# Group normalization on one core: a one-tile VectorE loop, a quartered last store, and longer runs of stores and loads

## The chip, the cores and the metric

The kernel runs on 1 core of a Trainium2 chip. The metric is the time of one execution on the device, in microseconds (us). Kernels are compared only within the same rounds.

Beside the profile page and its views I use two kinds of records that lie in the same trace: one for each packet that a DMA engine moved (start, duration, size), and one for each of the 16 completions that a transfer reports. "us as a mean of 16" means that the engines' lost times were added and divided by 16.

## The reference

```python
# x: [128, 1024, 32, 16] bf16; g, b: [1024] bf16; 32 groups of 32 channels
xr  = x.reshape(B, 32, C // 32, H, W)
mu  = xr.mean(axis=(2, 3, 4), keepdims=True)
var = ((xr - mu) ** 2).mean(axis=(2, 3, 4), keepdims=True)
xn  = (xr - mu) / jnp.sqrt(var + 1e-5)
return xn.reshape(B, C, H, W) * g[None, :, None, None] + b[None, :, None, None]
```

One (image, group) pair fills one partition with 16384 values. A tile is 128 such pairs, 4 MB, and there are 32 tiles. Each is loaded once and stored once: 134 MB in, 134 MB out.

## The kernel before

Six tiles (slots) lie in SBUF at a time. SyncE issues all loads and stores on one queue, in runs: two stores, then two loads, then three and three.

```python
def on_sync(e):
    def load(j):                       # needs the slot's last store to have landed
        if j >= SLOTS:
            e.wait_ge(st[j % SLOTS], 16 * (j // SLOTS))
        e.dma_start(out=slot(j), in_=x_v[j]).then_inc(ld[j % SLOTS], 16)
    def store(i):                      # needs VectorE to have finished the tile
        e.wait_ge(done[i % SLOTS], i // SLOTS + 1)
        e.dma_start(out=o_v[i], in_=slot(i)).then_inc(...)
    for j in range(SLOTS):
        load(j)
    for i in range(NT):
        store(i)
        if i % RUN == FIRST_RUN - 1:   # RUN = 3, FIRST_RUN = 2
            for j in range(max(SLOTS, i + 1 + SLOTS - RUN), min(i + 1 + SLOTS, NT)):
                load(j)
```

For each tile TensorE sums 12 of 32 chunks, VectorE sums the other 20 by pairs ("the pair sum"; for the last tile TensorE sums all 32 and VectorE none), ScalarE forms the mean and then the squares, and VectorE normalizes in place with 32 instructions. VectorE's loop is unrolled over the six slots, with fixed addresses:

```python
def one(c, turn):                      # VectorE
    ...
    if follows:
        pair(*then)                    # pair sum of the next tile, waits for its load
    e.wait_ge(stded[c], turn)
    ...                                # 1/std, scale, bias: three small instructions
    for k in range(KC):                # 32 x tensor_scalar, 128 x 512
        ...
    ts.then_inc(done[c], 1)            # releases the store
```

## Time and profile before

| | before |
|---|---|
| time, median of the first 3 runs | 632.77 us (632.59 to 633.53) |
| span of the profiled execution | 630.3 us |
| data moved | 268.48 MB |
| duration of a 32 KB packet, at the 1st and at the 90th percentile | 1.213 us |
| VectorE per tile when it does not wait | 16.55 us |
| load plus store of a tile at the steady rate | 19.4 us |

These lines are from the page of the kernel before: the span, each engine's busy time with its share of the span, then, over 40 slices of 15.8 us, the mean busy share of the 16 DMA engines in tenths and what they moved in GB/s, and the share of the DMA queues.

```profile
span 630.3 us, 2508 instructions
...
PE 157.6 (25%) x405; PEld 52.0 (8%) x405; DVE 522.3 (83%) x1185; ACT 504.0 (80%) x258; POOL 0.8 (0%) x6
...
DMA  8999999999999999999999999999999999999996
GB/s 366 433 431 416 433 433 434 430 433 435 435 435 433 430 433 433 435 433 435 433 433 428 433 433 426 433 433 437 430 433 433 433 428 433 433 433 429 433 410 285
...
q1 hardware_dynamic: 9216, 268.44, 99.0%
```

VectorE is busy for 83% of the span, ScalarE for 80%, and the DMA engines for 99%. The rate stands at 433 GB/s in nearly every slice. No 32 KB packet of this trace took less than 1.213 us. The 8192 of them are 512 for each of the 16 engines, which is 621.1 us at 1.213 us each; with a first packet at 2.0 us there is little left to win while packets take that long.

One tile in VectorE's timeline (start, duration, instruction, count):

```profile
51.45 0.20 DVE L253 RECIPROCAL rstd<-std 128x1 f32<-128x1 f32 x1
51.69 0.24 DVE L255 TENSOR_SCALAR scl<-gb,rstd 128x32 f32<-128x32 f32 x1
51.96 0.25 DVE L259 SCALAR_TENSOR_TENSOR bia<-scl,nm,gb 128x32 f32<-128x32 f32 x1
52.25 10.43 DVE L268 TENSOR_SCALAR ring<-ring,scl,bia 128x512 bf16<-128x512 bf16 x32
62.59 5.49 DVE L236 SCALAR_TENSOR_TENSOR jp<-ring 128x5120 fp8e5<-128x5120 bf16 x1
```

The pair sum of the next tile starts at 62.59, before the last normalizing instruction has ended at 62.68: there is no gap between tiles.

The end, in the view of windows (from, to, length, busy us and instruction count of each engine, clock, DMA share, GB/s):

```profile
605.00:610.00 5.00, 0.00 (x0) 0.00 (x0) 4.76 (x16) 0.10 (x1) 0.00 (x0) 0.50 1.03 446
610.00:615.00 5.00, 0.00 (x0) 0.00 (x0) 5.00 (x17) 0.00 (x0) 0.00 (x0) 0.50 0.74 321
615.00:620.00 5.00, 0.00 (x0) 0.00 (x0) 1.33 (x5) 0.00 (x0) 0.00 (x0) 0.50 0.80 341
620.00:625.00 5.00, 0.00 (x0) 0.00 (x0) 0.00 (x0) 0.00 (x0) 0.00 (x0) 0.50 0.99 426
```

There is a dip from 613.5 to 617.5 us, worth 2.55 us as a mean of 16: the last tile is finished at 616.4 and most engines have nothing to store before that. But the 16 completions of one transfer are spread over 0.7 us at the beginning of the execution and over 5.5 us at the end. The store before the last is complete on the median engine at 614.2 us and on the slowest at 619.4. The slowest one has no dip, and it ends the execution.

### The profile page before, as it was taken

Reading aid. Unit: us, or ns where it says so; the run is one execution under the profiler, and the core shown is the slowest. Engines: PE = TensorE matmul, PEld = TensorE weight load, DVE = VectorE, ACT = ScalarE, POOL = GpSimd, SP = SyncE. Lnnn points to the kernel's source line nnn. Section 1 sums busy time; section 2 is a strip of 40 time slices with the busy share of each in tenths; the row PEclk is TensorE's granted clock in tenths of the full one; section 3 lists DMA queues with packets and bytes.
Section 4 is the critical chain, followed back from the end, with each engine's and each line's share of the span. In section 5 each row is a group of like instructions: output and inputs, shape, how many; then the busy total and the mean of one; then the engine's idle time right before and its main releaser. Section 6 shows DMA issues by size and latency. Waiting matters only on the chain.

```text
span 630.3 us, 2508 instructions
## 1 busy us (share of the span) xinstructions
PE 157.6 (25%) x405; PEld 52.0 (8%) x405; DVE 522.3 (83%) x1185; ACT 504.0 (80%) x258; POOL 0.8 (0%) x6
## 2 busy tenths in 40 slices
PE   1453205005302320250052015203510450065000
PEld 0110001001100100010010001001100110012000
DVE  1579999999996998599589949994997799499671
ACT  0799999999996999399859958993999399769930
POOL 0000000000000000000000000000000000000000
PEclk9867656556655665665566556655665665567555
DMA  8999999999999999999999999999999999999996
GB/s 366 433 431 416 433 433 434 430 433 435 435 435 433 430 433 433 435 433 435 433 433 428 433 433 426 433 433 437 430 433 433 433 428 433 433 433 429 433 410 285
DMA packets 9316, 268.48 MB, mean 426 GB/s; under 512 B 1120, under 2 KB 1120, under 8 KB 1120
## 3 DMA queue, kind: packets, MB, share of 16 engines
q1 hardware_dynamic: 9216, 268.44, 99.0%
q8 instruction: 1, 0.02, 0.0%
q14 instruction: 3, 0.02, 0.0%
q10 hardware_dynamic: 96, 0.00, 0.0%
HBM read 134.22 MB, written 134.22 MB: 426 GB/s over the span
## 4 chain that ended last, share of the span: by engine, by line
DMA 63%; DVE 26%; ACT 7%; issue 0%; SPq 0%; DVEq 0%
DMA out_dram<-ring 43%; DMA ring<-in_x_dram 20%; DVE ring L268 16%; DVE jp L236 9%; ACT ja L203 7%; DVE bia L259 0%; DVE scl L255 0%; ACT jm L195 0%; SPq L123 0%; ACT var L213 0%; DVE rstd L253 0%; ACT std L217 0%; DVEq L275 0%; SPq L309 0%; SPq L278 0%
## 5 line engine op out<-in xcount | busy, mean ns | idle before, releaser
L203 ACT ACTIVATE ja<-ring,nm 128x8192 fp8e5<-128x8192 bf16 x64 | 455.9, 7123 | 2.1
L268 DVE TENSOR_SCALAR ring<-ring,scl,bia 128x512 bf16<-128x512 bf16 x1024 | 333.7, 408 | 1.2
L173 PE MATMUL ps<-ring,eye 128*128 128x512 bf16 x404 | 157.4, 571 | 411.8 <-DMA ring<-in_x_dram 411.8
L236 DVE SCALAR_TENSOR_TENSOR jp<-ring 128x5120 fp8e5<-128x5120 bf16 x31 | 170.1, 5488 | 63.8 <-DMA ring<-in_x_dram 63.8
L195 ACT ACTIVATE jm<-ps 128x513 fp8e5<-128x513 f32 (+1 forms) x32 | 19.2, 601 | 95.0 <-DVE jp L236 95.0
L173 PEld LDWEIGHTS ps<-ring,eye 128*128 128x128 bf16 x404 | 51.9, 134 | 516.9 <-issue 467.2
L253 DVE RECIPROCAL rstd<-std 128x1 f32<-128x1 f32 x32 | 6.3, 198 | 15.5 <-ACT std L217 15.5
L203 ACT ACTIVATION_READ_ACCUMULATOR ja<-ring,nm 128x1 f32 x64 | 12.0, 187 | 0.0
L217 ACT ACTIVATE std<-sq,var 128x1 f32<-128x1 f32 x32 | 9.4, 295 | 1.0
L213 ACT ACTIVATE var<-sq,eps_t 128x1 f32<-128x1 f32 x32 | 9.4, 295 | 1.0
L259 DVE SCALAR_TENSOR_TENSOR bia<-scl,nm,gb 128x32 f32<-128x32 f32 x32 | 8.0, 251 | 1.1
L255 DVE TENSOR_SCALAR scl<-gb,rstd 128x32 f32<-128x32 f32 x32 | 7.7, 241 | 1.1
L231 DVE COPY gb<-gb_p 128x64 f32<-128x64 f32 x1 | 0.2, 225 | 10.1 <-PE gb_p L167 10.1
L195 ACT ACTIVATION_READ_ACCUMULATOR jm<-ps 128x1 f32 x32 | 6.2, 194 | 0.0
L236 DVE DVE_READ_ACCUMULATOR jp<-ring 128x1 f32 x31 | 4.4, 143 | 0.0
L167 PE MATMUL gb_p<-gb_b,rep 32*128 32x64 bf16 x1 | 0.2, 205 | 11.2 <-DMA gb_b<-in_b_dram 11.2
L188 ACT ACT_TABLE_LOAD x1 | 1.3, 1283 | 1.9 <-issue 1.9
L224 DVE MEMSET ones_b<- 128x128 bf16 x1 | 0.2, 165 | 1.1 <-SPq L278 1.1
L167 PEld LDWEIGHTS gb_p<-gb_b,rep 32*128 32x128 bf16 x1 | 0.1, 100 | 11.1 <-issue 11.1
L146 POOL TENSOR_SCALAR_AFFINE_SELECT rep<-ones_b 32x128 bf16<-32x128 bf16 x1 | 0.3, 304 | 0.0
L142 POOL TENSOR_SCALAR_AFFINE_SELECT eye<-ones_b 128x128 bf16<-128x128 bf16 x1 | 0.3, 295 | 0.9 <-DVEq L226 0.9
L188 ACT ACTIVATE warm<-eps_t 128x1 f32<-128x1 f32 x1 | 0.2, 203 | 0.0
(5 smaller groups left out, 0.5 us busy)
## 6 DMA issues: line engine op xcount, KB each, us to landing
ring<-in_x_dram SPq DMA_DIRECT2D x32, 4096.0 KB, 29.1
out_dram<-ring SPq DMA_DIRECT2D x32, 4096.0 KB, 33.9
gb_b<-in_g_dram ACTq DMA_DIRECT2D x1, 2.0 KB, 6.4
gb_b<-in_b_dram ACTq DMA_DIRECT2D x1, 2.0 KB, 9.6
```

Of the source, the lines that this page charges most:

```text
L167: e.matmul(out=gb_p[:], lhsT=rep[:], rhs=gb_b[:], start=True, stop=True).then_inc(s_gbp, 1)
L173: mm = e.matmul(out=sums(c), lhsT=eye[:], rhs=slot(c)[:, k * MM_FREE : (k + 1) * MM_FREE], start=(k == 0), stop=(k == chunks - 1),)
L188: e.activation(out=warm[:], in_=eps_t[:], func=ACT.Sqrt)
L195: e.activation(out=jm[:, 0 : src.shape[1]], in_=src, func=ACT.Identity, scale=-inv_n, accum_out=nm[:, c : c + 1], saturate=False,).then_in ...
L203: e.activation(out=ja[:], in_=slot(c)[:, h * (F // 2) : (h + 1) * (F // 2)], func=ACT.Square, bias=nm[:, c : c + 1], scale=1.0, accum_out= ...
L213: e.activation(out=var[:], in_=sq[:, 0:1], func=ACT.Identity, bias=eps_t[:], scale=inv_n).then_inc(varred[c], 1)
L217: e.activation(out=std[:, c : c + 1], in_=sq[:, 1:2], func=ACT.Sqrt, bias=var[:], scale=inv_n).then_inc(stded[c], 1)
L236: e.scalar_tensor_tensor(out=jp[:], in0=slot(c)[:, first : first + w], scalar=1.0, in1=slot(c)[:, first + w : first + 2 * w], op0=ALU.mult ...
L253: e.reciprocal(out=rstd[:], in_=std[:, c : c + 1]).then_inc(inverted[c], 1)
L255: e.tensor_scalar(out=scl[:], in0=gb[:, 0:KC], scalar1=rstd[:], scalar2=None, op0=ALU.mult).then_inc(scaled[c], 1)
L259: e.scalar_tensor_tensor(out=bia[:], in0=scl[:], scalar=nm[:, c : c + 1], in1=gb[:, KC : 2 * KC], op0=ALU.mult, op1=ALU.add,).then_inc(shi ...
L268: ts = e.tensor_scalar(out=a, in0=a, scalar1=scl[:, k : k + 1], scalar2=bia[:, k : k + 1], op0=ALU.mult, op1=ALU.add,)
```

## The change

Its intent: VectorE's loop shrinks to one tile, with the addresses of the 32 normalizing instructions computed in registers ahead of time, under the pair sum; the last store goes out in quarters, so that it starts before the tile is complete; and stores and loads alternate in longer runs, so that the queue changes direction (from loads to stores or back) less often. ScalarE and TensorE are looped in full too, TensorE's last matmul waits for the pair sum, and the pair sum waits for TensorE's first matmul instead of the load. The last tile is now treated like the others, with a pair sum on VectorE.

```diff
-TRIPS = 5
-RUN = 3
-FIRST_RUN = 2
+RUNS = (3, 4, 4, 4, 4, 4, 3, 6)
+NQ = 4
...
         def store(i):
-            e.wait_ge(done[i % SLOTS], i // SLOTS + 1)
-            e.dma_start(out=o_v[i], in_=slot(i)).then_inc(
-                st[i % SLOTS] if i + SLOTS < NT else s_fin, 16
-            )
+            w = F // store_parts(i)              # 4 parts for the last tile, else 1
+            for p in range(store_parts(i)):
+                e.wait_ge(done, NQ * i + NQ // store_parts(i) * (p + 1))
+                e.dma_start(
+                    out=o_v[i][:, p * w : (p + 1) * w], in_=slot(i)[:, p * w : (p + 1) * w]
+                ).then_inc(st[i % SLOTS] if i + SLOTS < NT else s_fin, 16)
...
-        for i in range(NT):
-            store(i)
-            if i % RUN == FIRST_RUN - 1:
-                for j in range(max(SLOTS, i + 1 + SLOTS - RUN), min(i + 1 + SLOTS, NT)):
-                    load(j)
+        i = 0
+        for run in RUNS:
+            for n in range(run):
+                store(i + n)
+            i += run
+            for j in range(i + SLOTS - run, min(i + SLOTS, NT)):
+                load(j)
...                                              # VectorE
-        pair(0, 1)
-        e.drain()
-        in_rounds(e, one)
+        pair(0)
+        with nc.Fori(0, NT, 1, engines=[e.engine]) as i:
+            with e.If(i < NT - 1):
+                e.drain()
+                pair(i + 1)
+            parts = [part(i, k * HW, HW) for k in range(KC)]
+            e.keepalive_nop([e.lower_ap(a) for a in parts])
+            e.wait_ge(stded, i + 1)
...
+            for k, a in enumerate(parts):
                 ts = e.tensor_scalar(
                     out=a, in0=a, scalar1=scl[:, k : k + 1], scalar2=bia[:, k : k + 1],
                     op0=ALU.mult, op1=ALU.add,
                 )
-            ts.then_inc(done[c], 1)
+                if (k + 1) % KQ == 0:
+                    ts.then_inc(done, 1)
```

More of the change, by code (lines that the diff above doesn't have):

```diff
@@ L53 @@
     NMM = F // MM_FREE
-    LOOPED = TRIPS * SLOTS
+    ROUNDS = -(-NT // SLOTS)
+    REST = NT - (ROUNDS - 1) * SLOTS
+    KQ = KC // NQ
     PAIRED = F - PE_CHUNKS * MM_FREE
-    assert SLOTS < NT and LOOPED < NT - 1 and NT - LOOPED <= SLOTS
+    ITEM = 2
+    assert NT > SLOTS and 0 < REST < SLOTS and sum(RUNS) == NT and RUNS[-1] == SLOTS
     assert F % MM_FREE == 0 and PAIRED % 2 == 0 and SLOTS % PS_BUFS == 0
@@ L94, in sems @@
         return [sem(f"{name}{c}") for c in range(SLOTS)]
-    ld, st, summed, paired, meaned, stded, done = (
-        sems(n) for n in ("ld", "st", "sum", "pair", "mean", "std", "done")
-    )
-    half, both, varred, inverted, scaled, shifted = (
-        sems(n) for n in ("half", "both", "var", "inv", "scl", "bia")
-    )
+    ld, st, summed, meaned = (sems(n) for n in ("ld", "st", "sum", "mean"))
+    half, both, varred = (sems(n) for n in ("half", "both", "var"))
+    inverted, scaled, shifted = (sem(n) for n in ("inv", "scl", "bia"))
+    first_in, paired, stded, done = (sem(n) for n in ("first", "pair", "std", "done"))
     s_gb, s_ones, s_eye, s_gbp, s_fin = (
@@ L105, with store_parts @@
     )
+    def store_parts(i):
+        return NQ if i == NT - 1 else 1
     def slot(i):
@@ L114, in sums_and_pairs @@
         return ps[:, c % PS_BUFS * 2 * MM_FREE : c % PS_BUFS * 2 * MM_FREE + MM_FREE + 1]
-    def pairs(c):
-        return ps[:, (c % PS_BUFS * 2 + 1) * MM_FREE : (c % PS_BUFS * 2 + 1) * MM_FREE + 1]
     def on_sync(e):
@@ L125, in store @@
         def store(i):
-            e.wait_ge(done[i % SLOTS], i // SLOTS + 1)
-            e.dma_start(out=o_v[i], in_=slot(i)).then_inc(
-                st[i % SLOTS] if i + SLOTS < NT else s_fin, 16
-            )
+            w = F // store_parts(i)
[4 more added lines that the diff above has]
+                ).then_inc(st[i % SLOTS] if i + SLOTS < NT else s_fin, 16)
         for j in range(SLOTS):
             load(j)
-        for i in range(NT):
-            store(i)
-            if i % RUN == FIRST_RUN - 1:
-                for j in range(max(SLOTS, i + 1 + SLOTS - RUN), min(i + 1 + SLOTS, NT)):
-                    load(j)
-        e.wait_ge(s_fin, 16 * SLOTS)
-    def on_gpsimd(e):
-        e.wait_ge(s_ones, 1)
+        i = 0
[5 more added lines that the diff above has]
+                load(j)
+        e.wait_ge(s_fin, 16 * sum(store_parts(i) for i in range(NT - SLOTS, NT)))
+    def on_gpsimd(e):
+        e.memset(ones_b[:], 1.0)
+        e.memset(eps_t[:], EPS)
+        e.drain()
+        e.sem_inc(s_ones, 1)
+        for c in range(SLOTS - 2, SLOTS):
+            e.sem_inc(meaned[c], 1)
         e.affine_select(
@@ L153, in in_rounds @@
     def in_rounds(e, one):
-        with nc.Fori(0, TRIPS, 1, engines=[e.engine]) as t:
-            for c in range(SLOTS):
-                one(c, t + 1)
-        for c in range(NT - LOOPED):
-            one(c, TRIPS + 1)
-    def is_last(c, turn):
-        return isinstance(turn, int) and LOOPED + c == NT - 1
+        with nc.Fori(0, ROUNDS, 1, engines=[e.engine]) as t:
+            for c in range(REST):
+                one(c, t)
+            with e.If(t < ROUNDS - 1):
+                for c in range(REST, SLOTS):
+                    one(c, t)
     def on_tensor(e):
@@ L167, in on_tensor, with one @@
         e.matmul(out=gb_p[:], lhsT=rep[:], rhs=gb_b[:], start=True, stop=True).then_inc(s_gbp, 1)
-        def one(c, turn):
-            e.wait_ge(meaned[(c - PS_BUFS) % SLOTS], turn)
-            e.wait_ge(ld[c], turn * 16)
-            chunks = NMM if is_last(c, turn) else PE_CHUNKS
-            for k in range(chunks):
+        def one(c, t):
+            for k in range(PE_CHUNKS):
+                if k == 0:
+                    e.wait_ge(ld[c], (t + 1) * 16)
+                elif k == PE_CHUNKS - 2:
+                    e.wait_ge(meaned[(c - 2) % SLOTS], t + 1)
+                elif k == PE_CHUNKS - 1:
+                    e.wait_ge(paired, t * SLOTS + (c + 1))
                 mm = e.matmul(
@@ L177, in one @@
                     start=(k == 0),
-                    stop=(k == chunks - 1),
+                    stop=(k == PE_CHUNKS - 1),
                 )
+                if k == 0:
+                    mm.then_inc(first_in, 1)
             mm.then_inc(summed[c], 1)
@@ L188, in on_scalar, with one @@
         e.activation(out=warm[:], in_=eps_t[:], func=ACT.Sqrt)
-        def one(c, turn):
-            if not is_last(c, turn):
-                e.wait_ge(paired[c], turn)
-            e.wait_ge(summed[c], turn)
-            src = sums(c) if is_last(c, turn) else sums_and_pairs(c)
+        def one(c, t):
+            e.wait_ge(summed[c], t + 1)
             e.activation(
-                out=jm[:, 0 : src.shape[1]], in_=src, func=ACT.Identity, scale=-inv_n,
+                out=jm[:], in_=sums_and_pairs(c), func=ACT.Identity, scale=-inv_n,
                 accum_out=nm[:, c : c + 1], saturate=False,
             ).then_inc(meaned[c], 1)
-            e.wait_ge(meaned[c], turn + (1 if c >= PS_BUFS else 0))
-            for h in range(2):
-                if h == 1:
-                    e.wait_ge(half[c], turn)
+            for h, (ready, at) in enumerate(
+                ((meaned[c], t + (2 if c >= SLOTS - 2 else 1)), (half[c], t + 1))
+            ):
+                e.wait_ge(ready, at)
                 e.activation(
@@ L210, in one @@
                     saturate=False,
-                ).then_inc(both[c] if h == 1 else half[c], 1)
-            e.wait_ge(both[c], turn)
+                ).then_inc((half, both)[h][c], 1)
+            e.wait_ge(both[c], t + 1)
             e.activation(
@@ L215, in one @@
             ).then_inc(varred[c], 1)
-            e.wait_ge(varred[c], turn)
+            e.wait_ge(varred[c], t + 1)
             e.activation(
                 out=std[:, c : c + 1], in_=sq[:, 1:2], func=ACT.Sqrt, bias=var[:], scale=inv_n
-            ).then_inc(stded[c], 1)
+            ).then_inc(stded, 1)
         in_rounds(e, one)
     def on_vector(e):
-        e.memset(ones_b[:], 1.0)
-        e.memset(eps_t[:], EPS)
-        e.drain()
-        e.sem_inc(s_ones, 1)
-        for c in range(PS_BUFS, SLOTS):
-            e.sem_inc(meaned[c], 1)
+        bytes_of_ring = ring[:].bitcast(mybir.dt.uint8)
@@ new lines, in part, with pair @@
+        def part(i, lo, n):
+            at = (i % SLOTS) * (F * ITEM) + lo * ITEM
+            return bytes_of_ring[:, bass.ds(at, n * ITEM)].bitcast(BF16)
+        def pair(i):
+            lo, n = PE_CHUNKS * MM_FREE, PAIRED // 2
+            e.wait_ge(first_in, i + 1)
+            e.scalar_tensor_tensor(
+                out=jp[:],
+                in0=part(i, lo, n),
+                scalar=1.0,
+                in1=part(i, lo + n, n),
+                op0=ALU.mult,
+                op1=ALU.add,
+                accum_out=ps[:, bass.ds((i % PS_BUFS) * (2 * MM_FREE) + MM_FREE, 1)],
+                saturate=False,
+            ).then_inc(paired, 1)
@@ L230, in on_vector @@
         e.wait_ge(s_gbp, 1)
         e.tensor_copy(out=gb[:], in_=gb_p[:])
-        def pair(c, turn):
-            first, w = PE_CHUNKS * MM_FREE, PAIRED // 2
-            e.wait_ge(ld[c], turn * 16)
-            e.scalar_tensor_tensor(
-                out=jp[:],
-                in0=slot(c)[:, first : first + w],
-                scalar=1.0,
-                in1=slot(c)[:, first + w : first + 2 * w],
-                op0=ALU.mult,
-                op1=ALU.add,
-                accum_out=pairs(c),
-                saturate=False,
-            ).then_inc(paired[c], 1)
@@ L247, in one @@
-        def one(c, turn):
-            follows = not isinstance(turn, int)
-            then = (c + 1) % SLOTS, turn + (c + 1) // SLOTS
-            if follows:
-                pair(*then)
-            e.wait_ge(stded[c], turn)
-            e.reciprocal(out=rstd[:], in_=std[:, c : c + 1]).then_inc(inverted[c], 1)
-            e.wait_ge(inverted[c], turn)
+        pair(0)
+        with nc.Fori(0, NT, 1, engines=[e.engine]) as i:
+            with e.If(i < NT - 1):
+                e.drain()
+                pair(i + 1)
+            parts = [part(i, k * HW, HW) for k in range(KC)]
+            e.keepalive_nop([e.lower_ap(a) for a in parts])
+            e.wait_ge(stded, i + 1)
+            e.reciprocal(out=rstd[:], in_=std[:, bass.ds(i % SLOTS, 1)]).then_inc(inverted, 1)
+            e.wait_ge(inverted, i + 1)
@@ L255, in one @@
             e.tensor_scalar(
                 out=scl[:], in0=gb[:, 0:KC], scalar1=rstd[:], scalar2=None, op0=ALU.mult
-            ).then_inc(scaled[c], 1)
-            e.wait_ge(scaled[c], turn)
+            ).then_inc(scaled, 1)
+            e.wait_ge(scaled, i + 1)
             e.scalar_tensor_tensor(
-                out=bia[:], in0=scl[:], scalar=nm[:, c : c + 1], in1=gb[:, KC : 2 * KC],
-                op0=ALU.mult, op1=ALU.add,
-            ).then_inc(shifted[c], 1)
-            e.wait_ge(shifted[c], turn)
@@ L264, in one @@
-            for k in range(KC):
-                if k == 1 and follows:
-                    e.wait_ge(paired[then[0]], then[1])
-                a = slot(c)[:, k * HW : (k + 1) * HW]
+                out=bia[:], in0=scl[:], scalar=nm[:, bass.ds(i % SLOTS, 1)],
+                in1=gb[:, KC : 2 * KC], op0=ALU.mult, op1=ALU.add,
+            ).then_inc(shifted, 1)
+            e.wait_ge(shifted, i + 1)
+            for k, a in enumerate(parts):
                 ts = e.tensor_scalar(
@@ L271, in one @@
                 )
-            ts.then_inc(done[c], 1)
-        pair(0, 1)
-        e.drain()
-        in_rounds(e, one)
+                if (k + 1) % KQ == 0:
+                    ts.then_inc(done, 1)
     with tc.tile_critical(no_gpsimd_drain=True):
```

## The prediction

> **What bounds it now.** The transfers. The page shows the 16 DMA engines 99% busy (queue part), at 433 to 435 GB/s in nearly every slice[...]. The trace's packet records: 8192 packets of 32 KB, 1.213 us each at the 1st to 90th percentile, 512 per engine, 621.1 us of pure moving. The first starts at about 2.0 us and the span is 630.3, so only some 7 us are lost. VectorE needs 16.55 us a tile (timeline: pair sum 5.5, 32 normalizing instructions 10.4, three small ones), ScalarE 15.9, load plus store 19.4.
>
> **The tail.** The stretches show 331 GB/s at 610 to 620 and 275 at 620 to 630: the last store is issued at 616.4 and lands 12.7 us later. Packet records have 12 of 16 engines idle for about 4 us before it (2.6 us as a mean of 16). But the engines are not level. [...]here the 16 completions of one transfer spread over 0.7 us at the start and 5.5 us at the end. The store before the last completes on the median engine at 614.2, on the last at 619.4; that straggler never goes idle, and ends the run.
>
> **The change.**
> 1. Quartered last store: fills the gap of the engines ahead. Worth 2.6 us if engines were level; on the straggler nothing (perhaps +0.1 us for four times as many packets).
> 2. Runs of 4: seven instead of nine switches from loads to stores. Transfers land 9.67 to 9.71 us apart in either direction, so the rate stays. But the straggler's lag grows by about 0.3 us per switch (slow packets of 1.3 to 2.1 us stand there): two fewer, -0.7 us. Slack shrinks: I reckon that the third store must be issued by 80 us (now 79.2), the seventh by 148 (now 145.5).
> 3. VectorE's loop: a drain, a branch and the pair's addresses stand in the open between tiles. Register operations took 40 to 63 ns, branches 50 to 72 ns in this trace: estimate 0.5 us a tile. The 32 addresses[...] hide under the pair sum. Period 17.1 us, still under 19.4.
> 4. The mean waits for a last matmul after the pair sum: about +0.5 us, in ScalarE's slack; the first store comes at 47 instead of 46.2 us, off the path.
>
> With 0.5 us a tile the third store is ready near 81, the seventh near 149.5: small gaps on the engines ahead, hidden from the straggler (1.9 to 2.5 us behind there). Much changes off the critical path, little on it.
>
> **Predicted: 632.0 us**, 630.2 to 635.8 eight times in ten. Faster by over 2%: 1% (621 us of moving forbid it). Within 2%: 93%. Slower: 6%.
>
> **What would show it.** Span 628 to 631; DMA share still 99%; VectorE period 17.0 to 17.3 in the saturated early stretch; no dip of GB/s just before the last store; a completion spread of still 3 to 6 us at the end.
>
> **What would make it wrong.** Addresses not hidden, or slower normalizing instructions: past 1 us a tile, each further 0.1 us costs 0.6 us at the seventh store; at 3 us VectorE is the limit and the time passes 645. Or the straggler's lag hangs on something that the change removes (instruction fetches at 45 and 106 us coincide with two of its steps): then the quartered store's 2.6 us comes too, near 629. The three runs of before already span 0.9 us.

Numbers of the traces: VectorE's branches in the kernel before took 47 to 72 ns, its register operations 40 to 63; a matmul there took 0.571 us in the mean, which is the size of point 4's +0.5 us. The deadlines of point 2 and the thresholds of the last paragraph are estimates, from the landings 9.67 to 9.71 us apart and from 16.55 and 19.4 us a tile.

## The result, and the profile after

| | before | after |
|---|---|---|
| time, median | 632.68 us (632.24 to 633.53, 4 runs) | 635.58 us (635.26 to 635.62, 4 runs) |
| ratio, 95% interval | | 1.0043 (1.0026 to 1.0060) |
| span | 630.3 us | 633.9 us |

The change is within 2%, but the difference is clear of noise: 2.9 us slower between the medians.

The same lines of the page of the changed kernel:

```profile
span 633.9 us, 2973 instructions
...
PE 156.9 (25%) x380; PEld 50.1 (8%) x385; DVE 529.4 (84%) x1185; ACT 504.0 (80%) x258; POOL 1.0 (0%) x8
...
DMA  8999999999999999999999999999999999999996
GB/s 364 430 430 428 432 364 430 401 436 432 418 438 422 430 430 430 434 436 434 430 430 438 432 436 430 428 432 432 436 434 432 430 428 434 434 434 430 432 430 273
...
q1 hardware_dynamic: 9648, 268.44, 98.9%
```

The row of tenths shows nothing. The row of GB/s does: 364 in the sixth slice (79 to 95 us), then 401, 418 and 422 in the eighth, eleventh and thirteenth. After 206 us it is as steady as before. So the loss of the engines as a whole is made early, and not in the steady state.

Where each kernel stands after the same number of transfers, from the completion records (median of a transfer's 16 completions; in brackets the spread from its first to its last):

```
transfer no.   before          after           after - before
 8             81.8 (1.9)      81.6 (0.7)      -0.2
 9             91.2 (2.1)      93.6 (0.7)      +2.4
12            120.4 (2.9)     123.7 (0.7)      +3.3
16            159.2 (2.9)     163.1 (0.3)      +3.9
20            197.8 (2.9)     202.2 (0.6)      +4.4
24            236.6 (3.3)     241.4 (0.5)      +4.8
40            391.6 (4.2)     396.4 (1.4)      +4.8
62            604.6 (5.5)     609.3 (4.2)      +4.7
last completion of all        629.1   632.5    +3.4
```

On the median engine everything is lost between the 8th and the 24th transfer. The slowest engine, which sets the end, gives another picture. By the last of the 16 completions after the 8th transfer, the changed kernel's slowest engine is 1.5 us ahead of the other's (81.9 us against 83.4), after the 9th 0.9 behind, after the 24th 2.0 and after the 62nd 3.2 (613.0 against 609.7). Its early lead and its later loss, from the 40th on, come from the lag between the engines and not from a gap. The first step, 2.4 us, is a queue that ran dry. Windows of the two kernels around 80 us; first before:

```profile
74.00:78.00 4.00, 0.00 (x0) 0.00 (x0) 4.00 (x14) 3.97 (x3) 0.00 (x0) 0.50 0.99 426
78.00:82.00 4.00, 0.00 (x0) 0.00 (x0) 4.00 (x5) 4.00 (x1) 0.00 (x0) 0.50 0.95 410
82.00:86.00 4.00, 0.00 (x0) 0.00 (x0) 3.89 (x7) 3.19 (x7) 0.00 (x0) 0.50 1.06 459
```

then after:

```profile
74.00:78.00 4.00, 2.08 (x5) 0.45 (x3) 4.00 (x14) 4.00 (x1) 0.00 (x0) 0.74 1.06 459
78.00:82.00 4.00, 0.00 (x0) 0.00 (x0) 3.90 (x13) 3.97 (x3) 0.00 (x0) 0.69 0.61 262
82.00:86.00 4.00, 0.00 (x0) 0.00 (x0) 3.60 (x1) 4.00 (x1) 0.00 (x0) 0.50 0.93 393
```

The DMA share falls to 0.61. (A window counts a packet whole where it starts, so single shares can pass 1.) The packet records put the gap at 81.0 to 83.0 us, 1.53 us as a mean of 16. SyncE's timeline (start, duration from the first to the last instruction of the row, count) names the transfer that came late:

```profile
64.70 17.57 SPq L129 DMA_DIRECT2D out_dram<-ring  x2
82.31 12.07 SPq L123 DMA_DIRECT2D ring<-in_x_dram  x3
99.16 0.34 SPq L129 DMA_DIRECT2D out_dram<-ring  x1
```

The row at 64.70 is the second and the third store; the third was issued at 81.93, when the six loads and two stores before it were through. The run of 3 stores puts this third store before the first of the following loads, and those can't start without it. In the kernel before, two loads stand in front of it and it is wanted only near 100 us.

Why is it at 81.93 and not at 79 us? VectorE's timeline of one tile, answering to the one shown before:

```profile
47.94 5.49 DVE L243 SCALAR_TENSOR_TENSOR jp<-ring 128x5120 fp8e5 x1 [0.50 <-issue]
53.35 0.14 DVE L243 DVE_READ_ACCUMULATOR jp<-ring  x1
53.35 0.20 DVE L264 RECIPROCAL rstd<-std 128x1 f32 x1
53.59 0.24 DVE L266 TENSOR_SCALAR scl<-gb,rstd 128x32 f32<-128x32 f32 x1
53.96 0.25 DVE L270 SCALAR_TENSOR_TENSOR bia<-scl,nm,gb 128x32 f32<-128x32 f32 x1
```

VectorE now stands idle for 0.50 us before each pair sum ("issue": nothing that the profile shows was waited for), and the bias instruction starts 0.37 us after the scale instruction instead of 0.27. The period is 17.24 us instead of 16.55. The first store goes out at 47.46 instead of 46.16, because the first pair sum waits for a matmul and the mean for another one. So the third store is late by 1.30 + 2 x 0.69 = 2.7 us.

The rest of the loss, from 93 to 241 us, is not idle time. In the packet records there are clusters of slow packets, of 1.3 to 2.3 us instead of 1.213, one or two for nearly every engine (in all 13 packets at 160 us, 25 to 28 in each of the others): at 91 us (0.90 us as a mean of 16), 120 us (0.84), 160 us (0.29) and 199 us (0.71), 2.74 us together. They stand where the queue changes between loads and stores. The kernel before passes its switches in that stretch with at most 0.05 us each. Both kernels share two earlier clusters, at the first packets (0.65) and at the first switch near 60 us (0.8). Gap and clusters, 1.53 + 2.74 = 4.3 us, are most of the 4.7 us by which the median engine is later at the 62nd transfer. At the end 1.3 us of it come back, because the slowest engine is behind the first by only 4.2 us instead of 5.5.

The chain of work that ended last, by engine, before and then after, is a warning:

```profile
DMA 63%; DVE 26%; ACT 7%; issue 0%; SPq 0%; DVEq 0%
```

```profile
ACT 54%; DMA 21%; DVE 11%; issue 7%; PE 3%; DVEq 2%; SPq 0%
```

Read alone, this would say that ScalarE has become the limit. It has not: it is busy for the same 504.0 us, and experiment a_runs3 below, with the same ScalarE code, is as fast as the kernel before. The chain starts at the last quarter's store, which waited for VectorE, and from there it finds waits of compute on compute all the way back, while the DMA queue beside it was full.

### The profile page after: what moved, and what is told of

It reads as the page before. It is cut to its first block, busy times and chain, and to the rows that moved or that the text cites. A ratio compares the mean times of both kernels' runs of the same rounds, so it can differ in the third digit from the quotient of the medians.

```text
span 633.9 us, 2973 instructions
## 1 busy us (share of the span) xinstructions
PE 156.9 (25%) x380; PEld 50.1 (8%) x385; DVE 529.4 (84%) x1185; ACT 504.0 (80%) x258; POOL 1.0 (0%) x8
## 4 chain that ended last, share of the span: by engine, by line
ACT 54%; DMA 21%; DVE 11%; issue 7%; PE 3%; DVEq 2%; SPq 0%
ACT ja L213 50%; DMA ring<-in_x_dram 21%; DVE ring L276 9%; PE ps L184 3%; ACT jm L205 2%; DVEq L259 1%; ACT var L223 1%; ACT std L227 1%; DVE jp L243 1%; DVEq L262 0%; SPq L129 0%; DVE bia L270 0%; DVE scl L266 0%; DVEq L264 0%; DVEq L243 0%
## 5 line engine op out<-in xcount | busy, mean ns | idle before, releaser
L276 DVE TENSOR_SCALAR ring<-ring,scl,bia x1024 | 333.5, 406 | 1.2
L243 DVE SCALAR_TENSOR_TENSOR jp<-ring 128x5120 fp8e5 (+1 forms) x32 | 175.7, 5492 | 64.2 <-PE ps L184 52.2
L205 ACT ACTIVATE jm<-ps 128x513 fp8e5<-128x513 f32 x32 | 19.3, 602 | 101.9 <-PE ps L184 101.9
L184 PEld LDWEIGHTS ps<-ring,eye 128*128 128x128 bf16 x384 | 50.0, 137 | 534.4 <-DVE jp L243 322.3
L264 DVE RECIPROCAL rstd<-std 128x1 f32 x32 | 6.3, 196 | 11.9 <-ACT std L227 11.9
L243 DVE DVE_READ_ACCUMULATOR jp<-ring (+1 forms) x32 | 4.5, 140 | 0.0
```

What stands on the lines that cost most here:

```text
L184: mm = e.matmul(out=sums(c), lhsT=eye[:], rhs=slot(c)[:, k * MM_FREE : (k + 1) * MM_FREE], start=(k == 0), stop=(k == PE_CHUNKS - 1),)
L205: e.activation(out=jm[:], in_=sums_and_pairs(c), func=ACT.Identity, scale=-inv_n, accum_out=nm[:, c : c + 1], saturate=False,).then_inc(me ...
L243: e.scalar_tensor_tensor(out=jp[:], in0=part(i, lo, n), scalar=1.0, in1=part(i, lo + n, n), op0=ALU.mult, op1=ALU.add, accum_out=ps[:, bas ...
L264: e.reciprocal(out=rstd[:], in_=std[:, bass.ds(i % SLOTS, 1)]).then_inc(inverted, 1)
L276: ts = e.tensor_scalar(out=a, in0=a, scalar1=scl[:, k : k + 1], scalar2=bia[:, k : k + 1], op0=ALU.mult, op1=ALU.add,)
```

## The experiments

Theory T: the third store comes too late and the queue runs dry at 81 us; the gap itself and the costly direction switches that follow it are the loss. Rivals: R1, longer runs cost by themselves; R2, the new loops or the quarters cost by themselves; later R3 to R5, told at each run. All kernels below gave correct results.

| run | median us | ratio to before (95%) | gaps, mean of 16 | clusters within 150 us after it, sum |
|---|---|---|---|---|
| a_runs3 | 632.57 | 0.9993 (0.9979 to 1.0007) | none | |
| b_runs4 | 633.19 | 1.0002 (0.9988 to 1.0016) | none | |
| a_first2 | 640.05 | 1.0111 (1.0096 to 1.0127) | 4.75 at 129 us, 5.48 at 610 us | 1.61 |
| b_quarter | 633.23 | 1.0003 (0.9990 to 1.0017) | none | |
| b_runs4_slow | 635.01 | 1.0026 (1.0012 to 1.0040) | 0.37 at 81 us | 1.82 |
| a_ease | 636.35 | 1.0050 (1.0036 to 1.0063) | 4.80 at 556 us | 1.84 |
| b_late | 636.21 | 1.0054 (1.0041 to 1.0068) | 2.15 at 71 us | 3.03 |
| b_fifteen | 638.87 | 1.0083 (1.0070 to 1.0097) | (the end itself) | |
| a_ease2 | 632.72 | 1.0005 (0.9991 to 1.0019) | none | |
| a_onestore | 637.49 | 1.0078 (1.0064 to 1.0091) | 1.44 at 81 us, 5.84 at 618 us | 2.80 |
| b_late_split | 638.09 | 1.0084 (1.0070 to 1.0098) | 2.70 at 71 us | 1.96 |
| b_gap_late | 636.06 | 1.0044 (1.0030 to 1.0057) | 4.34 at 410 us | 1.59 |

The dip of the kernel before at 613 us (2.55) is not counted as a gap; it recurs in b_runs4 (2.63), b_runs4_slow (2.77), b_late (1.23), b_late_split (1.71) and b_gap_late (0.43), while in a_first2 and a_onestore the last entry stands at its place. Gaps and clusters are read from the packet records of each run's profiled execution. They are means over the engines; the end is set by the slowest one, so their sum is not the loss in time.

### The runs and the loop, each alone: a_runs3 and b_runs4

a_runs3 is the changed kernel with the old order of the transfers:

```diff
-RUNS = (3, 4, 4, 4, 4, 4, 3, 6)
+RUNS = (2, 3, 3, 3, 3, 3, 3, 3, 3, 6)
```

> The changed kernel with the run lengths of before (2, then eight of 3, then the last six). Theory T (the third store comes too late, because VectorE's period grew to 17.24 us, and this empties the queue for 1.5 us at 81 us and puts all 16 engines in step, so that the next direction switches cost 0.3 to 0.8 us each): with this order the third store is needed only near 100 us, so no gap; 630.5 to 632.5 us. Rival R2 (the new loops, or the quartered store, cost by themselves): stays at 635 to 636.

b_runs4 is the kernel before with the new order:

```diff
-        for i in range(NT):
-            store(i)
-            if i % RUN == FIRST_RUN - 1:
-                for j in range(max(SLOTS, i + 1 + SLOTS - RUN), min(i + 1 + SLOTS, NT)):
-                    load(j)
+        i = 0
+        for run in (3, 4, 4, 4, 4, 4, 3, 6):
+            ...                                  # as in the change
```

> The kernel before with the run lengths of the change (3, five of 4, 3, last six) and nothing else. Theory T: VectorE at 16.55 us a tile has the third store ready at 79.2, in time for the queue that runs out near 81.6, so no gap: 632 to 633 us. Rival R1 (longer runs cost by themselves): 634.5 to 636.

Measured: 632.57 and 633.19 us, both the same as before. Neither part costs anything alone, and together they cost 2.9 us. R1 and R2 fall: it is an interaction. In a_runs3 VectorE's period is 17.24 us as in the changed kernel, so the slower loop is harmless where the store isn't wanted early. In b_runs4 the third store is issued at 79.0 us and the queue doesn't run dry. Its windows, to be held against the changed kernel's 0.61 and 0.93:

```profile
78.00:82.00 4.00, 0.00 (x0) 0.00 (x0) 4.00 (x4) 4.00 (x1) 0.00 (x0) 0.50 0.91 393
82.00:86.00 4.00, 0.00 (x0) 0.00 (x0) 3.89 (x8) 3.19 (x7) 0.00 (x0) 0.50 0.99 426
```

b_runs4 also tests the saving that I had claimed for fewer switches. It has seven switches from stores to loads instead of nine (and eight from loads to stores instead of ten; the prediction names the wrong direction, but the difference is two either way), and the completions near the end spread over 5.6 us, as before (5.5). There is no saving.

### The smallest repair, tried carelessly: a_first2

```diff
-RUNS = (3, 4, 4, 4, 4, 4, 3, 6)
+RUNS = (2, 4, 4, 4, 4, 4, 4, 6)
```

> The changed kernel with a first run of 2 instead of 3, then six of 4, last six. Theory T: no gap at the third store, 630.5 to 632.5 us, as good as the runs of 3. Rival R1 (runs of 4 cost): 635 to 636.

Measured: 640.05 us. The miss is mine: with this order the store of tile 5 is wanted by about 129 us, and VectorE finishes it at 133.5. The profile of this run shows the dry queue:

```profile
125.00:130.00 5.00, 2.30 (x7) 0.69 (x5) 5.00 (x17) 5.00 (x1) 0.00 (x0) 0.82 0.81 347
130.00:135.00 5.00, 0.00 (x0) 0.00 (x0) 4.50 (x12) 4.97 (x3) 0.00 (x0) 0.52 0.25 105
```

A second gap of 5.48 us stands before the last tiles. The run does not speak for R1, since b_runs4 has runs of 4 too. It shows that gaps are what to look for, and that clusters follow a gap here also (0.88 us at 143 us, 0.73 at 181).

### The quarters alone: b_quarter

```diff
+            parts = 4 if i == NT - 1 else 1
+            w = F // parts
+            for p in range(parts):
+                e.wait_ge(done[i % SLOTS], i // SLOTS + 1 + p)
+                e.dma_start(
+                    out=o_v[i][:, p * w : (p + 1) * w], in_=slot(i)[:, p * w : (p + 1) * w]
+                ).then_inc(st[i % SLOTS] if i + SLOTS < NT else s_fin, 16)
...
+                if is_last(c, turn) and (k + 1) % (KC // 4) == 0:
+                    ts.then_inc(done[c], 1)
```

> The kernel before with the last store in quarters and nothing else. My prediction's reading (the end is set by the engine that is 5 us behind and never goes idle): within 0.4 us of before, 632.2 to 633.2. Rival (the gap of 2.6 us before the last store is lost time of the kernel): 630 to 630.5.

Measured: 633.23 us, the same. The end of this run, to be held against the windows of the kernel before:

```profile
610.00:615.00 5.00, 0.00 (x0) 0.00 (x0) 5.00 (x17) 0.00 (x0) 0.00 (x0) 0.50 0.90 387
615.00:620.00 5.00, 0.00 (x0) 0.00 (x0) 1.88 (x6) 0.00 (x0) 0.00 (x0) 0.50 1.00 423
620.00:625.00 5.00, 0.00 (x0) 0.00 (x0) 0.00 (x0) 0.00 (x0) 0.00 (x0) 0.50 0.75 318
```

The dip of 321 and 341 GB/s is filled, and in exchange the engines that were ahead are idle at the end (from 623 to 626.5 us, 2.42 us as a mean of 16). The slowest engine is 6.0 us behind the first and ends as late as ever. A visible idle stretch of most engines was worth nothing.

### The changed kernel with one last store: a_onestore

```diff
-        return NQ if i == NT - 1 else 1
+        return 1
```

> The changed kernel with its last store in one piece. In it the last tile is finished near 623.4 us, and the engine that lags finishes the store before near 622.6. So here, unlike in the kernel before, the one piece comes too late for that engine too: some 2 us more than the changed kernel, 637 to 638. If quartering is worth nothing here as in the kernel before: 635.3 to 635.9.

Measured: 637.49 us, ratio 1.0078 against the changed kernel's 1.0043. So in the changed kernel the quarters are worth 0.0035 of 633 us, about 2.2 us. There VectorE finishes the last tile at 623.5 us instead of 616.4, too late for the slowest engine as well. By the trace of the changed kernel, 4.0 us of these 7 are there before its last three tiles; the rest comes in them, from the longer period and from the last tile's pair sum, which the kernel before did not have on VectorE. So the quarters pay where the last tile comes late, and gain nothing where it is in time. The slower loop alone does not make it late: in a_ease2 below, with the same loop and another order, the last quarter is issued at 616.3 us.

### Making the lateness by other means: b_runs4_slow

The kernel before with the new order, and VectorE slowed on purpose:

```diff
+        def lose(c, n):
+            e.tensor_scalar(
+                out=jp[:, 0:n], in0=slot(c)[:, 0:n], scalar1=1.0, scalar2=0.0,
+                op0=ALU.mult, op1=ALU.add, saturate=False,
+            )
+            e.drain()
...                                     # in one(c, turn)
+            if follows:
+                lose(c, 400)
...                                     # before the first pair sum
+        e.wait_ge(ld[0], 16)
+        lose(0, 1152)
```

> The kernel before with the runs of 4, and VectorE slowed on purpose by a copy of 400 elements and a drain in each looped tile (about 0.7 us) and by about 1.3 us once before the first pair sum, so that its stores come when the changed kernel's do. Nothing else of the change is in it. Theory T: the third store is issued near 82 us, the queue is empty for about 1.5 us, the next switches cost 0.3 to 0.9 us each: 635 to 636.5 us. Rival R3 (something else in the changed kernel, such as its loops' instructions, its other semaphores or the quarters, makes the loss): 632.5 to 633.5.

Measured: 635.01 us. VectorE's period became 17.0 us and the third store went out at 80.8 us, so the gap is only 0.37 us as a mean of 16. It was still followed by clusters of 0.97 us at 90 us and 0.85 at 119, and most of the loss is there: +1.8 us in the median against +2.9. R3 falls as the main cause: no line of the new loops is in this kernel. It also sets the deadline: a store issued at 79.0 us left no gap, one at 80.8 a small one, one at 81.9 a gap of 1.5 us.

### A gap in the old kernel with the old order: b_late

```diff
+        e.wait_ge(ld[0], 16)
+        for n in (PAIRED // 2, 4096):   # two throwaway sums, 10 us, once
+            e.scalar_tensor_tensor(
+                out=jp[:, 0:n], in0=slot(0)[:, 0:n], scalar=1.0, in1=slot(0)[:, n : 2 * n],
+                op0=ALU.mult, op1=ALU.add, saturate=False,
+            )
+            e.drain()
         pair(0, 1)
```

> The kernel before with its own runs, and two throwaway sums of together about 10 us on VectorE once, before the first pair sum: the second store comes near 72.7 us instead of 62.7, and is needed by about 70.7. A gap of about 2 us near 72 us, and none later (slack of later stores is over 10 us). If a gap makes the next switches costly by itself (theory T): costly switches of 0.3 to 0.9 us within the next 130 us, and 635 to 637 us in all. If only the gap counts (rival R5): no clusters of slow packets after it, and at most 2 us more than before, 633 to 635.

Measured: 636.21 us. The second store went out at 72.9 us. The windows of this run:

```profile
66.00:70.00 4.00, 2.64 (x7) 0.61 (x5) 4.00 (x14) 3.97 (x3) 0.00 (x0) 0.60 0.91 393
70.00:74.00 4.00, 0.00 (x0) 0.00 (x0) 4.00 (x10) 4.00 (x1) 0.00 (x0) 0.83 0.63 270
74.00:78.00 4.00, 0.00 (x0) 0.00 (x0) 4.00 (x1) 3.56 (x4) 0.00 (x0) 0.50 0.92 393
```

One gap of 2.15 us, and then clusters at the next four switches: 0.92 at 82 us, 0.75 at 101, 0.54 at 132 and 0.82 at 161. Nothing of the change is in this kernel. R5, that only the gap counts, falls: the clusters after it cost more than the gap.

### Does the slowest engine's lag hide a gap? b_gap_late

The prediction leaned on this: an engine that is behind has work left while the others are idle. The kernel before, with a longer delay later:

```diff
+        with nc.Fori(0, 3, 1, engines=[e.engine]) as t:
+            for c in range(SLOTS):
+                one(c, t + 1)
+        for n in 5 * [PAIRED // 2] + [1152]:     # throwaway sums, about 28.7 us, once
+            ...
+        with nc.Fori(3, TRIPS, 1, engines=[e.engine]) as t:
+            ...
```

> The kernel before with some 28.7 us of throwaway sums on VectorE once, before tile 18 (of 0 to 31), where its slack is larger: the store of tile 19 then comes near 412 us and is needed by about 409.7, so the queue runs empty for about 2 us near 410, as in b_late at 72. There the engine that lags is 4.2 us behind the median instead of 1.3. If the lag hides a gap (my prediction's reading) and the costly switches hit only engines in step: 632.5 to 633.7 us, the same as before. If a gap costs wherever it falls, as it did at 72 us: 635 to 637 us.

Measured: 636.06 us. The lag did hide the gap in the literal sense: the packet records show engines going idle from 410.3 us on, and one engine working through to 415.6, when the late store had already started on the others.

```profile
405.00:410.00 5.00, 0.00 (x0) 0.00 (x0) 5.00 (x17) 5.00 (x1) 0.00 (x0) 0.57 0.99 428
410.00:415.00 5.00, 0.00 (x0) 0.00 (x0) 5.00 (x16) 4.97 (x3) 0.00 (x0) 0.50 0.12 52
415.00:420.00 5.00, 0.00 (x0) 0.00 (x0) 5.00 (x3) 4.28 (x4) 0.00 (x0) 0.50 0.99 419
```

But the end came 3 us later. All engines restarted level (the spread of the next transfer's completions is 0.9 us, from 6.7), clusters followed at the next two switches (0.75 at 424 us, 0.84 at 452), and by the end the slowest engine was again 3.2 us behind the first. The 3 us are not all the gap's, though. The late store went out at 414.6 us instead of the planned 412, so the gap was 4.34 us and not about 2. And on the slowest engine of this profiled execution (the longest of the five) 2.4 us against the kernel before are there before the gap: its 42nd transfer ends at 417.3 us instead of 414.8. Of these, 0.8 us come between the 41st and the 42nd, where this run has an instruction fetch at 408.9 us that the kernel before has not; that the split loop's longer code brought it is not shown. A further 1.7 us come at the switch near 452 us. (The expectation puts that engine 4.2 us behind the median; in the trace of the kernel before it is 3.9 us behind the median at 411 us, and 4.2 behind the first.) So my reading that a gap is free while one engine lags is not borne out, since the slow packets after it reach that engine too, but what the gap itself cost is less than 3 us.

### Repairing the order: a_ease and a_ease2

```diff
-RUNS = (3, 4, 4, 4, 4, 4, 3, 6)
+RUNS = (2, 3, 4, 4, 4, 4, 4, 1, 6)     # a_ease
+RUNS = (2, 3, 4, 4, 4, 4, 3, 2, 6)     # a_ease2
```

> The changed kernel with runs of 2, 3, five of 4, 1, last six: the new loop, quarters and runs of 4 stay, but the third store is needed only near 100 us and no store of the second run before 120 us. Theory T: no gap, no costly switch, 632 to 633 us. Rival R4 (the new loop with runs of 4 loses wherever the runs start): 635 or more.

Measured: 636.35 us, a second planning error of mine. The run of 1 lets the last load wait for the landing of the only store in the queue: a gap of 4.80 us at 556 us, with clusters of 0.63 and 1.21 us just after it. Up to there this run had lost nothing: its 57th transfer completes at 556.4 us, and that of the kernel before at 556.2.

> The changed kernel with runs of 2, 3, four of 4, 3, 2, last six. The eased start of a_ease, without the run of 1 that made the last load wait for the only store in the queue (a gap of 4.8 us at 556 us, my mistake). Theory T: the queue never empties, no costly cluster but the first two that every kernel has, 632 to 633.5 us. Rival R4 (the new loop with runs of 4 loses anyway): 635 or more.

Measured: 632.72 us, the same as before, with the new loop, the quarters and runs of 4 all in it. Its only larger cluster past the first two is 0.40 us at 234 us. The row of GB/s on its page answers to the two shown above:

```profile
GB/s 366 432 432 424 434 432 432 434 432 434 430 432 430 434 424 432 434 432 434 432 432 430 432 432 430 432 432 434 432 430 432 434 432 426 434 426 432 432 431 255
```

R4 falls. An order that doesn't ask for the third store at 80 us is enough to repair the changed kernel. (The order differs near the end too, by a run of 2.)

### Two attempts at the mechanism below: b_late_split and b_fifteen

After the gap of the changed kernel the first 16 packets start within 0.14 us of each other (82.76 to 82.91 us). Is that why the next switches cost so much? b_late_split is b_late with a small transfer, 8 partitions of 16 KB, in the gap; the aim was to delay some of the engines by it:

```diff
+            if i == 1:
+                e.wait_ge(st[0], 16)
+                e.dma_start(
+                    out=slot(6)[0:8, 0 : F // 2], in_=x_v[6][0:8, 0 : F // 2]
+                ).then_inc(s_stag, 16)
             store(i)
+            if i == 1:
+                e.wait_ge(s_stag, 16)
```

> b_late with one more small transfer just before the late second store: 8 partitions of 16 KB of the next load[...]. If the costly switches after a gap come from all engines changing direction in step: the first cluster after the gap drops from 0.92 us to under 0.4, and the time to 633.5 to 635.5. If step has nothing to do with it: the clusters stay, 636 to 637.5 us.

Measured: 638.09 us (636.79 to 638.45), ratio 1.0084. The clusters shrank, from 3.03 to 1.96 us in sum, and the first at a switch from 0.92 to 0.52, not to under 0.4; the time did not follow and was higher than b_late's. Neither expectation was met. The test is weak, though: which engines a transfer of 8 partitions falls on is not shown, the small one took 0.75 to 1.82 us on its engines, not the 0.6 planned (an estimate, half of the 1.213 us of a 32 KB packet), the gap was longer than b_late's (2.70 against 2.15), and the profiled execution is one of two at 636.8 us, while the other three took over 638. There is evidence against a plain story of "in step" too: in a_runs3 the engines start their packets within 0.37 us of each other at 82 us and pass that switch and the next at no cost. Why the switches after a gap are costly stays open.

b_fifteen tries to spare the engine that lags. It has b_quarter's quarters, and the last two of them go out as 120 partitions and 8 partitions:

```diff
+                for lo, hi in ((0, 120), (120, 128)) if p > 1 else ((0, P),):
+                    e.dma_start(
+                        out=o_v[i][lo:hi, p * w : (p + 1) * w],
+                        in_=slot(i)[lo:hi, p * w : (p + 1) * w],
+                    ).then_inc(st[i % SLOTS] if i + SLOTS < NT else s_fin, 16)
```

> The kernel before with the quartered last store, its last two quarters each as one transfer of 120 partitions and one of 8. [...] If it is another one: no better than the plain quarters, 633.2 to 634.5.

An assumption of mine that no run shows: that the 120 partitions leave one of the 16 engines out. If that is the engine that lags, 629 to 630.5 us were expected; "another one" is the case that it is not.

Measured: 638.87 us, by the two ratios (1.0083 and 1.0003) some 5 us worse than the plain quarters, and outside both expectations. The two split quarters brought some 45 slow packets from 619 us on (0.4 to 1.5 us instead of 0.31; 1.2 us as a mean of 16), and the last small transfers ended at 635.1. Whether this form spared any engine the run doesn't tell; whatever it saved, it cost more. The hope was too high in any case: in b_quarter the second slowest engine is only 1.2 us ahead of the slowest, so sparing one engine could not have won more.

None of these versions beats both kernels. a_runs3, b_runs4, b_quarter and a_ease2 are as fast as the kernel before. What is left between it and 621.1 us of moving is mainly the start (2.0 us) and the lag of the slowest engine (5.5 us), and I found no experiment that removes the lag.

## Why the prediction was right or wrong

The time, 632.0 us with 630.2 to 635.8, holds the measured 635.58, but only 0.2 us below its upper edge, and the class (within 2%) was right. The sign was not: 0.8 us faster was forecast, 2.9 us slower measured. Since the step that was to decide the sign failed, as told below, it is the width of the range, and so in part luck, that made it hold.

- **"What bounds it now. The transfers."** Right. Four versions with different compute loops and orders end within 0.7 us of each other as long as the queue is full.
- **"Quartered last store: ... on the straggler nothing."** Right for the kernel before: b_quarter, 633.23 us. (The "+0.1 us for four times as many packets" is of the right size: in the changed kernel's trace an 8 KB packet takes 0.309 us, four of them 1.236 instead of 1.213, or 0.18 us over 8 packets, an engine's share of the last store's 128.) Incomplete for the changed one, where the last tile is 7 us later and the quarters save 2.2 us (a_onestore).
- **"Two fewer [switches], -0.7 us."** Wrong. b_runs4 has two fewer and the same lag and time. The steps in the lag that I had read as one per switch are not removed with the switch. That term should have been zero.
- **"Estimate 0.5 us a tile"** for VectorE's loop: the right mechanism in the main, mis-sized by a little. It measured 0.69: 0.50 us idle before the pair sum, and the rest partly because the pair sum no longer overlaps the last normalizing instruction by 0.09 us, partly the later bias instruction. Of what was to stand "in the open", the branches don't: in the tile shown they are over by 43.95 us, under the normalizing instructions, and what stands in the 0.50 us comes after the drain, which ends at 47.48. "The 32 addresses ... hide under the pair sum" was right: six packed register instructions of 76 to 131 ns each, done within 0.8 us of the pair sum's start. In the trace they run from 47.99 to 48.74 us, beside a pair sum that runs from 47.94 to 53.43.
- **"The first store comes at 47 instead of 46.2 us, off the path."** It came at 47.46, and it was on the path: those 1.3 us are half of the third store's lateness.
- **"The third store must be issued by 80 us ... ready near 81."** Right: it went out at 81.93 and left a gap.
- **"Small gaps on the engines ahead, hidden from the straggler (1.9 to 2.5 us behind there)."** This is the step that failed, twice over. In the changed kernel the completions were only 0.7 us apart at 82 us (against 1.9 before), so nothing was hidden. And in b_gap_late, where one engine works right through a gap, that engine still loses 1.7 us at a later switch: what counts are also the slow packets at the switches that follow, which I had not foreseen. A gap that was to cost nothing cost 1.53 us, and the slow packets after it 2.74, as means of 16.
- **"Instruction fetches at 45 and 106 us coincide with two of [the lag's] steps."** In the kernel before the fetches are at 44.2, 105.2 and 107.3 us, and the spread of completions grows from 0.7 to 2.1 us between 43 and 64 us and from 2.1 to 2.9 between 103 and 113. They are gone in the changed kernel, and with them the early lag (a spread of 0.7 us at 143 us), but not the late one: a_runs3 has no fetch either and ends with a spread of 5.4 us. The quarters' 2.6 us did not come.

## What to carry to other kernels

When the transfers are the limit, the order of the queue is a schedule with deadlines: write down for each store when the queue will run out in front of it and when its engine will have finished, above all in the first round, where nothing is ahead yet. A slower loop and a tighter order can each be free and cost together (here 632.57 and 633.19 us alone, 635.58 together). When a queue has run dry once, count also what comes after it: here the next two to four changes of direction cost 1.6 to 3.0 us more as a mean of 16, whether the gap was of 0.4 us or of 4.8. And before filling an idle stretch, check that the engine which ends last has it too: here b_quarter filled a dip of 2.55 us and took 633.23 us, the same as before.

## What the traces showed of the queue, the engines and the registers

- What a dry queue cost beyond the idle time: the changed kernel and each of the seven experiments with a gap in mid-run show clusters of packets of 1.3 to 2.4 us instead of 1.213 at the direction switches after it, 1.6 to 3.0 us as a mean of 16 in sum; full queues pass most switches with under 0.1 us (the first, near 60 us, cost 0.55 to 0.8 in every run, and the costliest later one was 0.40).
- The engines drift apart: in the kernel before, whose queue never empties before the last store, the spread of one transfer's completions grows from 0.7 to 5.5 us over 600 us, and the slowest engine sets the end. All large transfers are on one hardware queue there (q1 of the page), and the slowest engine is 5.5 us behind the first, with three more over 2 us behind. Which engines these are the records don't tell, and the cause is not shown.
- Register operations in front of an instruction took time: on VectorE of the changed kernel 76 to 133 ns for each of the six packed ones that make the addresses, and 0.50 us of idle time a tile before the pair sum, where a plain and two packed ones (40, 130 and 121 ns in the tile shown) stand behind a drain.
